# Splitting the first chunk's product at 288 tokens and regating four loads in a fused attention and ReLU-squared kernel

## Chip, cores and metric

The kernel runs on one core of one Trainium2 chip. The time is device time in microseconds (us). Before the change the median of 13 runs is 321.25 us (319.57 to 327.11). In the profiles, PE is TensorE's matrix multiply and PEld its weight load, DVE is VectorE, ACT is ScalarE, POOL is GpSimd and SP is SyncE, which here only issues DMAs.

## What is computed

Eight batch rows of attention, 576 tokens and 8 heads of 64 each, followed by a two-layer product with a squared ReLU between. Heads 0 to 3 see a sliding window of 32 tokens, heads 4 to 7 the same 32 places at a distance of four tokens.

```python
scores = scale * np.matmul(q, k.transpose(0, 1, 3, 2))
rel = pos[:, None] - pos[None, :]
mask_plain = (rel >= 0) & (rel < 32)
mask_dil = (rel >= 0) & (rel < 128) & (rel % 4 == 0)
attn = softmax(np.where(masks, scores, -1e9))
x = (attn @ v).transpose(0, 2, 1, 3).reshape(4608, 512)
h = x @ w_in                    # 512 x 2048
return np.maximum(h, 0.0) ** 2 @ w_out   # 2048 x 512
```

## The kernel before

The order of all instructions is written out by hand; each engine runs its own in that order, and waits on semaphores where data or a buffer is not there yet.

**Rows and chunks.** Attention goes by batch row `b` (576 tokens), the two products by chunk `c` (512 tokens). Chunk `c` can be multiplied once row `c` is done, so the product of chunk `b - 1` is interleaved with the attention of row `b`. A product is a Python generator in the list `pending`; `pump(n)` advances it by `n` steps, and TensorE's order is what these calls write down between the pieces of the attention.

**The products.** `mm1_gen` makes the hidden layer: for each of 16 columns of 128 of `w_in`, four matmuls over 512 tokens (L302) fill a PSUM tile `ph`, ScalarE's ReLU empties it into `rt` (L290), and VectorE squares two columns at once into `g` (L294). It yields twice a column. For chunk 0 the second product is `mm2_by_rows_gen` (64 matmuls, L323, in four blocks of `w_out`), for all later chunks `mm2_strassen_gen` (seven half-size products, L350, 28 steps), which needs sums of `g` that VectorE makes (L279 to L282) and differences of `w_out` (`weight_sums`, L271).

**Attention of rows 0 and 1.** `load_sliding_qk` brings q and k of the sliding heads to `sq` in float32, and `cast_sliding_qk` makes float16 of them; `load_dilated_qk` brings those of the dilated heads to `nd_` (the tile `early` in the profile). TensorE transposes them (`t_sliding` L475, `t_dilated` L489; the copies out of PSUM are L145 on ScalarE and L147 on VectorE), scores come from `s_sliding` (L514) and `s_dilated` (L551), each with an Exp on ScalarE (L504) and a mask on VectorE (L505). `av_sliding` (L583) and `av_dilated` (L597) multiply with v, VectorE normalizes (L565, L566), and `x_sliding` (L612) and `x_dilated` (L630) transpose the result into `xT`, the input of the first product, 288 tokens at a time. v comes as float32 in `sv` (6 loads of 256-byte pieces) and `sd` (2 loads), and is cast to `vp` and `vd`. Score and value tiles share two PSUM buffers (`papool`), everything else four (`pmool`): a third score tile waits for the Exp of the first.

**Rows 2 to 7.** q and k are copied in DRAM to float16 (`keep_qk`, tile `dk`, on GpSimd's queue), and `transpose_by_dma` brings them transposed to `QKTx` and `QKTd` (SP's queue, L194 and L196). `s_sliding_x` (L532) scores the sliding heads.

**Loads and who lets them go.** SP's queue carries, in this order, q and k of row 0 and v of row 0, q, k and v of row 1, v of row 2, the transposes of row 2, v of row 3 and so on. GpSimd's queue carries the dilated q and k, `w_in` (L128), `w_out` (L135), `dk` and the stores of the output; GpSimd also casts, so a load stands behind the casts that are written before it. `w_in` stands behind the first cast of row 0's v, `w_out` behind row 1's four casts of q and k (`cast_sliding_qk(1, (nc.gpsimd,) * 4)`). `dk` of row 2 stands behind `nc.gpsimd.memset(hold, 0.0)`, which waits for a VectorE write of `hold` made in the second value step of row 1; the loads of row 1 wait in the same way for two VectorE writes to `sq` and `nd_` (L698, L699).

**Order of the start.** Row 0's attention is filled with idle matmuls on zeros (`idle`, L450), which do nothing but keep TensorE going. Only after all of row 0 comes `mm1_gen(0)`: 22 steps alone, the other ten between the transposes and scores of row 1 (`begin(1, ...)`), then `mm2_by_rows_gen(0)` between the values of row 1. v of row 1 is cast on GpSimd.

Of the kernel before, what the change touches and what calls it, by code (L numbers as in the profile page):

```python
# [17 lines left out]
def kernel(  # L18
# [107 lines left out]
    def load_w_in():  # L126
        for f0, f1 in ((0, 1024), (1024, 2048)):
            nc.gpsimd.dma_start(  # L128
                out=wi[:, :, f0:f1],
                in_=moe_w_in[:, f0:f1].rearrange("(dh dl) f -> dl dh f", dl=P),  # L130
            )
# [17 lines left out]
    def cast_sliding_qk(b, engs):  # L149
        for i in (1, 0):  # L150
            for half in range(2):
                j0 = 3 * half
                copy(
                    engs[2 * i + half],
                    nq_[:, i, j0 : j0 + 3, :, :],
                    sq[:, i, :, D * j0 : D * (j0 + 3)].rearrange("p h (j d) -> p j h d", d=D),
                )

    def cast_sliding_v(eng, step, m0=0, m1=NB):
        for m in range(m0, m1, step):  # L160
            copy(eng, vp[:, m : m + step, :, 0:D], sv[:, m : m + step, :, :])

    def cast_dilated_v(eng, step):
        for t in range(2):
            for c in range(0, DIL, step):
                copy(
                    eng,
                    vd[:, t, c : c + step, :, 0:D],
                    sd[:, t, :, D * c : D * (c + step)].rearrange("p h (c d) -> p c h d", d=D),
                )  # L170

    def cast_v(eng):
        cast_sliding_v(eng, NB)
        cast_dilated_v(eng, DIL)
# [110 lines left out]
    def relu_squared(c, ffc, g, ph, rts):  # L285
        i, o = divmod(ffc, 2)
        if o == 0:
            rts[i] = osb.tile([P, 2, TOKC], FP16, name=f"rt{c}_{i}", tag="rt")
        rt = rts[i]
        nc.scalar.activation(rt[:, o, :], ph[:], ACTF.Relu)  # L290
        if i == NK - 1:
            nc.vector.tensor_mul(g[:, ffc, :], rt[:, o, :], rt[:, o, :])
        elif o == 1:
            nc.vector.tensor_mul(g[:, ffc - 1 : ffc + 1, :], rt, rt)  # L294

    def mm1_gen(c, g, sm=None):
        xs = xT[:, :, c * TOKC : (c + 1) * TOKC]
        rts = {}
        for ffc in range(NFF):
            ph = pmool.tile([P, TOKC], FP32, name=f"ph{c}_{ffc}", tag="pm")  # L300
            for dmk in range(NDM):
                nc.tensor.matmul(  # L302
                    ph,
                    wi[:, dmk, ffc * P : ffc * P + P],
                    xs[:, dmk, :],
                    start=(dmk == 0),
                    stop=(dmk == NDM - 1),
                )
# [129 lines left out]
    def hidden(c):  # L438
        return gp.tile([P, NFF, TOKC], FP16, name=f"g{c}", tag="g")
# [45 lines left out]

    def t_dilated(b, g, i, wide=False, eng=None):
        p_ = pt(f"pd{b}_{g}_{i}", wide)
        for j in range(6):
            nc.tensor.transpose(  # L489
                p_[:, QB * j : QB * (j + 1)],  # L490
                nd_[:, i, g, P * j : P * (j + 1)],
                ident[0:QB, 0:QB],
            )
        for a in range(2):
            copy(
                eng or (nc.vector if i else nc.scalar),
                QKTd[:, i, a, KPAD + 2 * g * CL : KPAD + 2 * (g + 1) * CL].rearrange(
                    "x (h p s) -> x h p s", h=2, s=3
                ),
                p_[:, 0:UW].rearrange("x (s a h p) -> x a h p s", a=2, h=2, p=48)[:, a],  # L500
            )
# [136 lines left out]
            py[:, 0:UW].rearrange("x (c r i) -> x c i r", c=2, r=DIL),  # L638
        )

    def begin(b, fill, wide=False):
        for hp in range(2):
            for i in (1, 0):
                t_sliding(b, hp, i, wide)
                fill()
        for g in range(2):
            s_sliding(b, g)
            fill()
            for i in (1, 0):
                t_dilated(b, g, i, wide, eng=nc.scalar)  # L650
                fill()
        for g in range(2):
            s_dilated(b, g)
            fill()

    def attn_values(b, fill, wide=False):
        xs = []
        for mp in range(3):
            xs.append(av_sliding(b, mp))
            fill()  # L660
        x_sliding(b, 0, xs, wide)
        fill()
        ys = [av_dilated(b, 0, 0)]
        fill()
# [10 lines left out]
        x_dilated(b, 1, zs, wide)  # L675


    cast_sliding_qk(0, (nc.scalar, nc.scalar, nc.vector, nc.gpsimd))
    cast_sliding_v(nc.gpsimd, 2, 0, 2)
    load_w_in()  # L680
    cast_sliding_v(nc.gpsimd, 2, 2, NB)
    cast_dilated_v(nc.gpsimd, 2)
    pj = pmool.tile([P, TOKC], FP32, name="pj", tag="pm")
    idle_matmuls(pj, 14, TOKC)
    n_idle = [0]

    def idle():
        n_idle[0] += 1
        idle_matmuls(pj, 5, P)

    begin(0, idle)

    def idle_and_load():
        idle()
        if n_idle[0] == 15:
            nc.vector.memset(sq[:, :, :, 0:1], 0.0)  # L698
            nc.vector.memset(nd_[:, :, :, 0:1], 0.0)  # L699

    attn_values(0, idle_and_load)
    load_sliding_qk(1)
    load_v(1)
    load_dilated_qk(1)
    cast_sliding_qk(1, (nc.gpsimd,) * 4)
    load_w_out()
    cast_sliding_v(nc.gpsimd, 2)
    cast_dilated_v(nc.gpsimd, 2)
    g0 = hidden(0)
    pending.append(mm1_gen(0, g0))  # L710
    pump(22)
    begin(1, lambda: pump(1))
    pump(1000)
    pending.append(mm2_by_rows_gen(0, g0))
    pump(4)
    n_val = [0]
    hold = const.tile([P, 1], FP32, name="hold")

    def rows_and_load():
        pump(2)  # L720
        n_val[0] += 1
        if n_val[0] == 2:
            nc.vector.memset(hold, 0.0)

    attn_values(1, rows_and_load, True)

    nc.gpsimd.memset(hold, 0.0)
    dk = keep_qk(2)
    load_v(2)
    transpose_by_dma(dk)  # L730
    pump(1000)
# [2 lines left out]
    for b in range(2, B):  # L734
        pending.append(moe_gen(b - 1))
        pump(1)
        if 2 < b < B - 1:
            dk = keep_qk(b + 1)
        if b == 2:

            for i in range(2):
                nc.gpsimd.tensor_copy(hold, QKTx[:, i, PADP + HH * S - 2 : PADP + HH * S - 1])
                nc.gpsimd.tensor_copy(hold, QKTd[:, i, 1, KPAD + S - 1 :])
            dk = keep_qk(b + 1)
            for _ in weight_sums():
                pump(2)
            cast_v(nc.scalar)
            load_v(b + 1)
            pump(4)
        else:  # L750
            pump(11)
        for g in range(2):
            s_sliding_x(b, g)
            pump(5)
        s_dilated(b, 0)
        pump(5 if b == 2 else 10)
        s_dilated(b, 1)
        if b + 1 < B:
            transpose_by_dma(dk)
        pump(4)  # L760
        attn_values(b, lambda: pump(2))
        if b + 1 < B:
            cast_v(nc.scalar)
        if b + 2 < B:
            load_v(b + 2)
        pump(1000)
# [33 lines left out]
```

## Time and profile before

| | us |
|---|---|
| median of 13 runs | 321.25 |
| the profiled execution, its own time | 320.37 |
| its span on the core | 318.2 |
| first product of chunk 0 begins | 28.04 |
| second product of chunk 0 begins | 50.32 |
| first product of chunk 1 begins (row 2's stage) | 68.22 |
| a row of the steady part (row 4, 134.6 to 166.5) | 31.9 |
| TensorE busy in it | 31.00 |

All times in the profile count from the start of the span. "Busy" is the time in which at least one instruction of an engine is under way; matmuls are pipelined, so the rate is read from the distance between them (one of 512 columns each 0.216 us at full clock). A number in square brackets behind a row of the timeline is the idle time of that engine before it, with what ended it. DMA shares are shares of 16 DMA engines; a share times the length of its window is called here the load's work, in us of all 16 engines.

### The profile page before, as it was taken

How to read it: one execution, taken by the hardware profiler on the slowest of the kernel's cores; microseconds unless marked ns; L12 is line 12 of the kernel's file. 1: busy time of each engine (PE TensorE's matmuls, PEld its weight loads, DVE VectorE, ACT ScalarE, POOL GpSimd, SP SyncE). 2: the span in 40 equal slices, each digit the busy share in tenths (PEclk: the TensorE clock that was granted, in tenths of full speed). 3: DMA queues.
4: the chain of work that ended last, by engine and by line, in shares of the span. 5: the costliest groups of instructions: out<-in, count | busy, mean ns of one | idle time of the engine just before them, and what ended most of it. 6: DMA issues, size and time to landing. Idle time of an engine off the chain costs nothing.

```text
span 318.2 us, 6930 instructions
## 1 busy us (share of the span) xinstructions
PE 297.8 (94%) x2876; PEld 195.2 (61%) x2876; DVE 212.0 (67%) x405; ACT 178.0 (56%) x302; POOL 47.9 (15%) x83
## 2 busy tenths in 40 slices
PE   6878887999999998999899989998999899999995
PEld 2866453544596457845784578447844784585484
DVE  4475576527987498748874887498749874844744
ACT  2565694168933982598259824982498236604620
POOL 4352590210202100030003000300000000000000
PEclk9599997999999999999999999999999999999999
DMA  7999999999997999199939992999330003003003
GB/s 187 234 181 225 213 194 202 238 204 232 226 205 179 221 207 191 24 266 204 197 39 268 206 182 50 268 196 203 38 135 0 2 2 132 0 2 132 2 0 132
DMA packets 83310, 47.89 MB, mean 150 GB/s; under 512 B 67792, under 2 KB 79568, under 8 KB 82896
## 3 DMA queue, kind: packets, MB, share of 16 engines
q1 hardware_dynamic: 75060, 26.12, 43.7%
q0 software_dynamic: 6848, 19.80, 28.2%
q10 hardware_dynamic: 1372, 1.54, 1.8%
q8 instruction: 22, 0.36, 0.5%
q14 instruction: 8, 0.07, 0.1%
HBM read 39.85 MB, written 16.52 MB: 177 GB/s over the span
## 4 chain that ended last, share of the span: by engine, by line
PE 71%; DVE 12%; ACT 7%; issue 4%; DMA 2%; POOL 2%; ACTq 0%; POOLq 0%
PE ph L302 32%; PE pob L350 9%; PE poa L350 6%; PE po L323 5%; PE poe L350 4%; PE poc L350 4%; DMA sq<-in_k_dram 2%; DVE AT L505 2%; PE paw L597 2%; ACT rt L290 2%; PE pod L350 2%; ACT QKTd L145 2%; ACT AT L504 2%; PE px L612 1%; DVE x_p L566 1%
## 5 line engine op out<-in xcount | busy, mean ns | idle before, releaser
L302 PE MATMUL ph<-xT,wi 128*128 128x512 f16 x576 | 131.2, 379 | 1.7 <-ACT rt L290 1.1
L290 ACT ACTIVATE rt<-ph 128x512 f16<-128x512 f32 x144 | 84.1, 606 | 28.3 <-PE ph L302 28.0
L302 PEld LDWEIGHTS <-wi 128*128 128x128 f16 x576 | 54.1, 98 | 63.4 <-issue 2.8
L294 DVE TENSOR_TENSOR g<-rt 128x1024 f16<-128x1024 f16 x63 | 45.0, 715 | 51.9 <-ACT rt L290 51.7
L350 PEld LDWEIGHTS <-sm 128*128 128x128 f16 x512 | 47.2, 98 | 5.0
L350 PEld LDWEIGHTS <-g 128*128 128x128 f16 x384 | 35.5, 98 | 5.3 <-DVE g L294 0.3
L618 ACT COPY xT<-px 128x576 f16<-128x576 f16 x16 | 10.2, 638 | 44.4 <-PE px L612 44.4
L350 PE MATMUL pob<-T,sm 128*128 128x256 f16 x256 | 32.5, 272 | 0.0
L350 PE MATMUL poa<-wo,g 128*128 128x256 f16 x256 | 31.9, 273 | 0.1
L370 POOL DMA_DIRECT2D out_dram<-otl x6 | 4.5, 756 | 159.2 <-DVE otl L405 140.7
L636 ACT COPY xT<-py 128x576 f16<-128x576 f16 x16 | 10.2, 638 | 30.1 <-PE py L630 30.1
L566 DVE TENSOR_TENSOR x_d<-paw,rcp_d 72x512 f16<-72x512 f32 x32 | 22.0, 686 | 1.1
L505 DVE TENSOR_TENSOR AT<-AT,maskp 128x576 f16<-128x576 f16 x32 | 17.5, 561 | 4.3 <-ACT AT L504 3.6
L504 ACT ACTIVATE AT<-ps 128x576 f16<-128x576 f32 x32 | 19.3, 664 | 0.6 <-PE ps L514 0.3
L504 ACT ACTIVATE AT<-pz 128x576 f16<-128x576 f32 x32 | 19.3, 681 | 0.0
L450 PE MATMUL pj<-zz 128*128 128x128 f16 (+1 forms) x124 | 16.5, 277 | 1.2 <-DVE zz L208 1.2
L323 PE MATMUL po<-wo,g 128*128 128x512 f16 x64 | 17.0, 402 | 0.0
L566 DVE TENSOR_TENSOR x_p<-pav,rcp_p 96x512 f16<-96x512 f32 x24 | 16.5, 687 | 0.8
L350 PE MATMUL poc<-T,sm 128*128 128x256 f16 x128 | 16.3, 272 | 0.0
L350 PE MATMUL pod<-T,g 128*128 128x256 f16 x128 | 16.1, 272 | 0.0
L350 PE MATMUL poe<-wo,sm 128*128 128x256 f16 x128 | 15.5, 273 | 0.0
L583 PE MATMUL pav<-vp,AT 128*128 128x65 f16 x192 | 10.1, 194 | 5.2 <-DVE x_p L566 4.5
(89 smaller groups left out, 328.0 us busy)
## 6 DMA issues: line engine op xcount, KB each, us to landing
sv<-in_v_dram SPq DMA_DIRECT2D x40, 128.0 KB, 8.7
sd<-in_v_dram SPq DMA_DIRECT2D x7, 512.0 KB, 10.9
dk<-in_k_dram POOLq DMA_DIRECT2D x12, 288.0 KB, 6.9
dk<-in_q_dram POOLq DMA_DIRECT2D x12, 288.0 KB, 8.8
out_dram<-otl POOLq DMA_DIRECT2D x6, 512.0 KB, 3.5
out_dram<-otu POOLq DMA_DIRECT2D x6, 512.0 KB, 4.3
wi<-in_moe_w_in_dram POOLq DMA_DIRECT2D x2, 1024.0 KB, 10.8
wo<-in_moe_w_out_dram POOLq DMA_DIRECT2D x4, 512.0 KB, 10.7
```

Of the source, the lines that this page charges most:

```text
L290: nc.scalar.activation(rt[:, o, :], ph[:], ACTF.Relu)
L294: nc.vector.tensor_mul(g[:, ffc - 1 : ffc + 1, :], rt, rt)
L302: nc.tensor.matmul(ph, wi[:, dmk, ffc * P : ffc * P + P], xs[:, dmk, :], start=(dmk == 0), stop=(dmk == NDM - 1),)
L323: nc.tensor.matmul(po, g[:, ffc, t * P : (t + 1) * P], wo[:, ffc, :], start=(ffc == 0), stop=(ffc == NFF - 1),)
L350: nc.tensor.matmul(acc, lhs[:, k, t * P : (t + 1) * P], rhs[:, k, :], start=(first and k == 0), stop=(k == NK - 1), skip_group_check=True,)
L450: nc.tensor.matmul(pj[:, 0:cols], zz[:, 0:P], zz[:, 0:cols], start=True, stop=True)
L504: nc.scalar.activation(AT[:, u, 0:UW], ps[:, :, 0 : UW // 2], ACTF.Exp, scale=scale)
L505: nc.vector.tensor_mul(AT[:, u, 0:UW], AT[:, u, 0:UW], mask)
L566: nc.vector.tensor_tensor(out=x[0:w], in0=pv[:, :, :, 0:D], in1=rcp[0:w].unsqueeze(3).to_broadcast([w, 2, HH, D]), op=ALU.mult,)
L583: nc.tensor.matmul(pav[:, i, h * (D + 2) : h * (D + 2) + D + 1], AT[:, u, off : off + P], vp[:, m, h, 0 : D + 1], start=True, stop=True,)
L618: nc.scalar.copy(xT[:, 0:2, t0 : t0 + 288], px[:, 0:UW].rearrange("x (c t) -> x c t", c=2),)
L636: nc.scalar.copy(xT[:, 2:4, t0 : t0 + 288].rearrange("x c (i r) -> x c i r", r=DIL), py[:, 0:UW].rearrange("x (c r i) -> x c i r", c=2, r= ...
```

## The change

The start is written anew; the functions of attention and of the later products stay, but for one new generator. `begin` becomes `transposes_and_scores` and `scores_dilated`.

- `mm1_part_gen` does the first product for a part of a chunk's tokens, one step a column. Chunk 0 goes in a part of 288 tokens, which is begun when the first 288 tokens of row 0 are in `xT`, and one of 224. The value steps of row 0 are reordered for it.
- `w_in` is let go by a VectorE write behind row 0's first two sliding masks, `w_out` by one behind the twelfth column of part one, `dk` and v of row 2 by writes in row 1's second value step (and `keep_qk(2)` moves into that step).
- Row 0's v is cast after `w_in` is issued, dilated heads first. Row 1's q and k are cast by ScalarE and VectorE after three columns of part two. Row 1's v is cast by ScalarE after the last column of part two and ahead of the Exp of row 1's dilated scores. Row 1's transposes use the four-buffer pool.
- In row 2's stage the sliding scores come four steps later (`pump(8)`), in rows 3 to 7 the second dilated score comes three steps sooner (7 for 10) and the values two steps later in all (9 for 4 behind it).

```diff
+    def mm1_part_gen(c, g, t0, t1):
+        xs = xT[:, :, c * TOKC + t0 : c * TOKC + t1]
+        rt = None
+        for ffc in range(NFF):
+            ph = pmool.tile([P, TOKC], FP32, name=f"ph{c}_{ffc}_{t0}", tag="pm")
+            for dmk in range(NDM):
+                nc.tensor.matmul(
+                    ph[:, 0 : t1 - t0],
+                    wi[:, dmk, ffc * P : ffc * P + P],
+                    xs[:, dmk, :],
+                    start=(dmk == 0),
+                    stop=(dmk == NDM - 1),
+                )
+            o = ffc % 2
+            if o == 0:
+                rt = osb.tile([P, 2, TOKC], FP16, name=f"rt{c}_{ffc}_{t0}", tag="rt")
+            nc.scalar.activation(rt[:, o, 0 : t1 - t0], ph[:, 0 : t1 - t0], ACTF.Relu)
+            if o == 1:
+                r = rt[:, :, 0 : t1 - t0]
+                nc.vector.tensor_mul(g[:, ffc - 1 : ffc + 1, t0:t1], r, r)
+            yield
...
-    cast_sliding_v(nc.gpsimd, 2, 0, 2)
-    load_w_in()
-    cast_sliding_v(nc.gpsimd, 2, 2, NB)
-    cast_dilated_v(nc.gpsimd, 2)
...
     def idle_and_load():
         idle()
-        if n_idle[0] == 15:
-            nc.vector.memset(sq[:, :, :, 0:1], 0.0)
-            nc.vector.memset(nd_[:, :, :, 0:1], 0.0)
-
-    attn_values(0, idle_and_load)
+        n_idle[0] += 1
+        if n_idle[0] == 5:
+
+            nc.vector.memset(hold, 0.0)
+            nc.gpsimd.memset(hold, 0.0)
+            load_w_in()
+            cast_dilated_v(nc.gpsimd, 2)
+            cast_sliding_v(nc.gpsimd, 2)
+
+    n_idle = [0]
+    transposes_and_scores(0, idle_and_load)
+    scores_dilated(0, idle)
+    xs = [av_sliding(0, 0)]
+    idle()
+    xs.append(av_sliding(0, 1))
+
+    nc.vector.memset(sq[:, :, :, 0:1], 0.0)
+    nc.vector.memset(nd_[:, :, :, 0:1], 0.0)
+    idle()
+    ys = [av_dilated(0, 0, 0)]
+    idle()
+    x_sliding(0, 0, xs, False)
+    idle()
+    ys.append(av_dilated(0, 0, 1))
+    idle()
+    xs.append(av_sliding(0, 2))
+    idle()
+    x_dilated(0, 0, ys, False)
     load_sliding_qk(1)
     load_v(1)
     load_dilated_qk(1)
-    cast_sliding_qk(1, (nc.gpsimd,) * 4)
+
+
+    g0 = hidden(0)
+    pending.append(mm1_part_gen(0, g0, 0, 288))
+    zs = []
+    for a in range(2):
+        pump(1)
+        zs.append(av_dilated(0, 1, a))
+    pump(1)
+    x_sliding(0, 1, xs, False)
+    pump(2)
+    x_dilated(0, 1, zs, False)
+    pump(8)
+    nc.vector.memset(hold, 0.0)
+    nc.gpsimd.memset(hold, 0.0)
     load_w_out()
-    cast_sliding_v(nc.gpsimd, 2)
-    cast_dilated_v(nc.gpsimd, 2)
-    g0 = hidden(0)
-    pending.append(mm1_gen(0, g0))
-    pump(22)
-    begin(1, lambda: pump(1))
     pump(1000)
+    pending.append(mm1_part_gen(0, g0, 288, TOKC))
+    pump(3)
+    cast_sliding_qk(1, (nc.scalar, nc.vector, nc.scalar, nc.vector))
+    pump(2)
+    transposes_and_scores(1, lambda: pump(1))
+    pump(1000)
+    cast_v(nc.scalar)
     pending.append(mm2_by_rows_gen(0, g0))
-    pump(4)
+    pump(3)
+    scores_dilated(1, lambda: pump(3))
     n_val = [0]
...
         if n_val[0] == 2:
             nc.vector.memset(hold, 0.0)
-
+            nc.vector.memset(sv[:, :, :, 0:1], 0.0)
+            nc.vector.memset(sd[:, :, :, 0:1], 0.0)
+            nc.gpsimd.memset(hold, 0.0)
+            dks.append(keep_qk(2))
+
+    dks = []
     attn_values(1, rows_and_load, True)
-
-    nc.gpsimd.memset(hold, 0.0)
-    dk = keep_qk(2)
+    dk = dks[0]
     load_v(2)
     transpose_by_dma(dk)
     pump(1000)
...
             cast_v(nc.scalar)
             load_v(b + 1)
-            pump(4)
+            pump(8)
...
         s_dilated(b, 0)
-        pump(5 if b == 2 else 10)
+        pump(5 if b == 2 else 7)
         s_dilated(b, 1)
         if b + 1 < B:
             transpose_by_dma(dk)
-        pump(4)
+        pump(4 if b == 2 else 9)
         attn_values(b, lambda: pump(2))
```

More of the change, by code (lines that the diff above doesn't have):

```diff
@@ L639, in x_dilated, with transposes_and_scores @@
         )
-    def begin(b, fill, wide=False):
+    def transposes_and_scores(b, fill):
         for hp in range(2):
             for i in (1, 0):
-                t_sliding(b, hp, i, wide)
+                t_sliding(b, hp, i)
                 fill()
@@ L649, in begin, with scores_dilated @@
             for i in (1, 0):
-                t_dilated(b, g, i, wide, eng=nc.scalar)
+                t_dilated(b, g, i, eng=nc.scalar)
                 fill()
+    def scores_dilated(b, fill):
         for g in range(2):
@@ L675, in attn_values @@
         x_dilated(b, 1, zs, wide)
+    hold = const.tile([P, 1], FP32, name="hold")
     cast_sliding_qk(0, (nc.scalar, nc.scalar, nc.vector, nc.gpsimd))
-    cast_sliding_v(nc.gpsimd, 2, 0, 2)
-    load_w_in()
-    cast_sliding_v(nc.gpsimd, 2, 2, NB)
-    cast_dilated_v(nc.gpsimd, 2)
     pj = pmool.tile([P, TOKC], FP32, name="pj", tag="pm")
     idle_matmuls(pj, 14, TOKC)
-    n_idle = [0]
     def idle():
-        n_idle[0] += 1
         idle_matmuls(pj, 5, P)
-    begin(0, idle)
     def idle_and_load():
         idle()
-        if n_idle[0] == 15:
-            nc.vector.memset(sq[:, :, :, 0:1], 0.0)
-            nc.vector.memset(nd_[:, :, :, 0:1], 0.0)
-    attn_values(0, idle_and_load)
+        n_idle[0] += 1
[23 more added lines that the diff above has]
+    x_dilated(0, 0, ys, False)
     load_sliding_qk(1)
@@ L704 @@
     load_dilated_qk(1)
-    cast_sliding_qk(1, (nc.gpsimd,) * 4)
-    load_w_out()
-    cast_sliding_v(nc.gpsimd, 2)
-    cast_dilated_v(nc.gpsimd, 2)
-    g0 = hidden(0)
-    pending.append(mm1_gen(0, g0))
-    pump(22)
-    begin(1, lambda: pump(1))
-    pump(1000)
+    g0 = hidden(0)
[11 more added lines that the diff above has]
+    nc.gpsimd.memset(hold, 0.0)
+    load_w_out()
+    pump(1000)
+    pending.append(mm1_part_gen(0, g0, 288, TOKC))
[5 more added lines that the diff above has]
+    cast_v(nc.scalar)
     pending.append(mm2_by_rows_gen(0, g0))
-    pump(4)
+    pump(3)
+    scores_dilated(1, lambda: pump(3))
     n_val = [0]
-    hold = const.tile([P, 1], FP32, name="hold")
     def rows_and_load():
```

## The prediction

> **What bounds the kernel now.** The page first: busy time, and the 40 slices of 8 us.
>
> ```profile
> PE 297.8 (94%) x2876; PEld 195.2 (61%) x2876; DVE 212.0 (67%) x405; ACT 178.0 (56%) x302; POOL 47.9 (15%) x83
> ...
> PE   6878887999999998999899989998999899999995
> ...
> DMA  7999999999997999199939992999330003003003
> ```
>
> TensorE is the bound from row 2 on; in the first six slices it has holes, while the DMA engines are full. So the start is read by the timeline, where each row gives start, duration, what, and the idle time before:
>
> ```profile
> 14.80 1.54 POOL L128 DMA_DIRECT2D wi<-in_moe_w_in_dram  x2
> ...
> 28.93 9.23 PE L302 MATMUL ph<-xT,wi 128*128 128x512 f16 x42 [0.29 <-ACT xT L636]
> ...
> 39.79 3.02 POOL L135 DMA_DIRECT2D wo<-in_moe_w_out_dram  x4
> ...
> 49.42 0.97 PE L551 MATMUL pz<-QKTd 64*128 64x72 f16 x16 [2.43 <-ACT AT L504]
> 50.32 3.16 PE L323 MATMUL po<-wo,g 128*128 128x512 f16 x8
> ...
> 77.38 0.43 PE L532 MATMUL ps<-QKTx 64*128 64x96 f16 x12
> ```
>
> At 49.42 TensorE had stood 2.43 us for the Exps of row 1's dilated scores. The windows of 3.41 us (busy of each engine, then clock, DMA share, GB/s) show what that cost:
>
> ```profile
> 46.07:49.48 3.41, 0.98 (x24) 0.52 (x23) 3.11 (x7) 3.41 (x10) 1.59 (x2) 1.00 1.18 191
> 49.48:52.90 3.42, 3.28 (x23) 1.37 (x23) 1.75 (x4) 1.59 (x3) 0.00 (x0) 0.50 1.22 198
> ```
>
> Half the clock in the next window: eight matmuls take 3.09 us in the chain of waits, 1.73 at full clock, some 1.5 us lost with the scores. Then the DMA queues while `w_out` (q0, GpSimd's) and row 2's v (q1, SP's) load together, 48 to 54:
>
> ```profile
> q0 software_dynamic: 928, 0.92, 90.8%
> q1 hardware_dynamic: 926, 0.23, 29.2%
> ```
>
> As many packets each, but v's are 256 bytes: `w_out` gets three parts in four. Last, what TensorE waits for from 102 to 290:
>
> ```profile
> PE pav L583 <- DVE x_p L566: 4.5, 5, 0.9
> PE ph L302 <- ACT rt L290: 0.6, 1, 0.6
> ```
>
> Once in each of rows 3 to 7 the third value tile waits 0.9 us for VectorE, which is late by its sums and masks.
>
> **The start, up to the last column of chunk 0.** `w_in` no longer waits for a cast of v but for two masks, which end at 15.5; with 0.4 us from a VectorE `hold` to a DMA behind it (55.76 to 56.13) it is issued at 15.9 instead of 14.8. It landed 13.5 us after issue at most, so by some 30. Row 0's values are paced by VectorE (0.85 us a tile, after the masks end at 21.6): the fourth is done at 25.5, `x_dilated` and its copy take 1.1, and part one begins at 26.65 instead of 28.04. Its matmuls have 288 columns, by the 512-column step of 0.216 us some 0.121 each, 0.485 a column. Four value and transpose pieces (0.27 each) lie between, so column 8 begins at 31.6, after `w_in`, and part one ends at 35.5. By then the kernel before had done 32 of its 64 matmuls (7.0 us of work), this one 7.8: the 288 tokens gain 0.8 us, no more, since they take the place of idle matmuls only from 26.65.
>
> Part two runs against ScalarE. Row 1's k landed by 35.8 and I take the same. From 37.1 ScalarE has 2 casts (1.56 for two at 7.60), 13 ReLUs of 224 columns (0.25 each; bounds 0.25 and 0.50, the latter the distance of 512-column ones at 81.1), 2 copies (0.54), 4 Exps (0.56) and 8 copies of 288 (0.32; four took 1.34 at 17.52): 10.6 us, and 0.7 for TensorE's waits, so 48.4. TensorE reaches `mm2` at 47.4 (its first block needs only four columns), does ten matmuls and the first dilated scores, and stands at 50.3 before the second: both score buffers wait for Exps, and these now stand behind the casts of row 1's v on ScalarE.
>
> **When row 1's v lands.** The twelfth column of part one ends at 33.6, VectorE squares it by 34.4, and `w_out` is issued at 34.7 instead of 39.79. Before, v had the engines nearly alone then. The loads' work (share times window, us of 16 engines):
>
> ```profile
> q0 software_dynamic: 2112, 2.10, 81.2%
> ...
> q1 hardware_dynamic: 3794, 1.50, 39.1%
> ```
>
> `w_out` (41 to 57): 13.0. One row of v (47 to 66): 7.4. Of v about 0.7 is done when `w_out` starts at 36.4 (its first packets came 1.7 after issue before). The 256-byte part, 3.7, goes at the 0.30 of the row above: until 48.7. `w_out` has then 1.9 left; the 1024-byte part shares with it (I take packet for packet, 0.47 and 0.70) to 51.4, and ends at 53.3. Together they need 20 at 1.2, which gives 53.1: as long as v is the one that waits, the end is fixed. Landing 0.6, the last cast 1.05 (77.18, two in 1.99), an Exp 0.6: TensorE goes on at 55.6. It has stood 5.3 us. Were v's share even, it would go on at 52.4 (casts of 3.4 from 48.4, then the Exp).
>
> From there 54 matmuls (11.7), the scores (0.3) and the eight value and four transpose pieces (2.8): 14.8. After so long a wait the clock is halved; at the start of the span, where matmuls resumed at 9.17, it stayed at half until about 15.3, so I take 4.2 us at half, 2.1 lost (bounds 0.9 and 3.4). Row 2's stage begins at 72.5 instead of 68.4: **+4.1** (+0.3 with even shares).
>
> The Trainium skill ("DMA: Bandwidth & Descriptors", "Rules for kernel authors") says to issue a DMA early and wait late. By that rule the earlier `w_out` costs nothing and the sum is that of the first rival. The rows speak against it, because the engines are shared and the earlier load is not the one that is waited for.
>
> **Row 2.** `dk` and v of row 2 are let go in the second value step, at 62.2 by the halved clock, instead of 56.13 for `dk` and 43.45 for v; between 53.3 and then the DMA engines have nothing to load. Before `QKTx` is there, they must do `dk` (5.7: 65.9% of 58 to 66.6), v (7.4; it is ahead of the transposes on SP's queue), the two stores of chunk 0 (3.5: 43.9% of 69 to 77) and some 6.6 of transposes (of 82.0% of 66 to 77.2, less v's share, two thirds): 23.2 at 1.15, from 63.9 until 84.1, and 0.9 to land. TensorE comes there after 12.5 columns (10.8) and the 0.9 that it waits behind the casts of v: 84.3. That is **+0.7** (0 to 2); `pump(8)` has bought the rest. At the end of the stage its four steps are missing as filler: the last values wait for VectorE 1.6 us and the copy 0.9. Against that stand holes that the earlier mm1 no longer has; my sum over the stage is **-0.2**. But 2.45 us of idle time in 2.75 is as much as halved the clock at 49.48; it may fall into two windows, so **+0.8** (0 to 1.7).
>
> The Trainium skill ("TensorE: Matmul & The Clock Gate", "What's actually happening") has the clock halved after an idle window of about 3.4 us. By that rule the 5.3 us halve it and the 2.45 don't, and the sum is 0.8 less; here 2.43 us with 0.98 busy in the window were enough, so I keep the term.
>
> **Rows 3 to 7.** The second dilated score comes 3 steps sooner, so its two masks (0.74 together at 153.47) fill VectorE's holes before the sums; the values come 2 steps (8 matmuls of 0.109, 0.87 us) later against the product. The 0.9 goes. At the end 8 matmuls instead of 16 cover ScalarE's casts of 3.4 us: the fifth `ph` of the next chunk would have had 0.8 us of slack and now waits about 0.15. Five times 0.75: **-3.7** (-4.5 to -2.5).
>
> GpSimd's casts (4.05 us for q and k, 0.65 each for v) go; they cost nothing but the waits already counted.
>
> **Sum.** 4.1 + 0.7 - 0.2 + 0.8 - 3.7 = +1.7 on the profiled span of 318.2 (its own time 320.37). The median is 0.9 over that run; the difference goes onto it: 322.95, say 323.0. By their bounds, the terms put this case at 321.0 to 325.5.
>
> **Rivals.**
> - *Faster: v lands in time.* If q1 gets an even share, or the small part flows ahead, TensorE goes on at 52.4 and the stage at 68.7; `dk` is let go near 57.5 and `QKTx` lands as TensorE arrives. 0.3 - 0.2 - 3.7 = -3.6: 317.6. For it: shares with 1024-byte pieces are unmeasured, v is split in two. Against: the 29.2%. It decides if v's last landing is before 50.
> - *Slower still: the steady rows don't gain.* If VectorE's sums move by as much as the values, or the next chunk's columns wait 0.9 for the casts, the 3.7 are lost: 326.7. For it: in row 3 the casts already cost 0.58 (105.91). Against: VectorE's holes of 0.6 us before the sums.
> - *It does not do what it says: `w_in` late.* Starting 1.1 later and meeting row 1's q, its second half could land at 33; column 8 waits 1.4, `w_out` is let go as much later, v comes sooner by about that: 321.5.
>
> **How the numbers follow.** The forecast 0.51, faster rival 0.31, slower 0.13, late `w_in` 0.05. A measurement here tells 0.3% (1.0 us) from no change. Of the forecast's case 0.09 lies within that, 0.42 above; of the late `w_in` 0.03 within, 0.02 on the faster side. Faster 0.33, same 0.12, slower 0.55. The range takes in both sides: 317.0 to 327.0, with some 0.1 left out at each end.
>
> **What would show it.** The second scores `pz` of row 1 with an idle time of about 5 us ended by an Exp, ScalarE waiting on `sv` and `sd`; the clock at half around 53 to 60; no wait of `pav` for `x_p` in rows 3 to 7; row 2's first product at about 72.5. If v lands before 50 or the steady rows are still 31.9 apart, the prediction is wrong.

## Result and profile after

The changed kernel takes 325.62 us (median of 11 runs, 321.59 to 336.12) against 320.91 us of the kernel before beside it (48 runs). The ratio is 1.0118, with a 95% interval of 1.0087 to 1.0149: slower by 0.9 to 1.5%. The ratio leaves out executions more than 1.5% above the fastest of the same kernel, so it lies below the quotient of the medians (1.0147). The profiled execution took 325.94 us with a span of 324.0, where the one before had 320.37 and 318.2.

The 5.8 us between the two spans, by stages (a row's stage begins with the first matmul of the first product that is interleaved with the row, that of the chunk before):

| stage | before, us | after, us | difference | forecast |
|---|---|---|---|---|
| start to row 2's stage | 68.22 | 72.59 | +4.37 | +4.1 |
| row 2's stage | 33.04 | 37.66 | +4.62 | +1.3 (0.7 - 0.2 + 0.8) |
| row 3's | 33.15 | 33.00 | -0.15 | -0.75 |
| rows 4 to 7, each | 31.95 | 31.19 | -0.76 | -0.75 |
| the rest | 55.98 | 56.00 | 0.0 | 0 |

("The rest" is what comes behind row 7's stage, the products of the last two chunks.) What TensorE waited for in the changed kernel, 40 to 115 us (in total, times, longest), and then 102 to 296:

```profile
PE pz L573 <- ACT AT L526: 5.1, 2, 4.9
PE ps L554 <- DMA QKTx<-dk: 2.3, 1, 2.3
PE py L652 <- DVE x_d L588: 1.1, 1, 1.1
```

```profile
PE py L652 <- DVE x_d L588: 1.1, 1, 1.1
PE ph L324 <- ACT rt L290: 0.6, 4, 0.2
PE ph L324 <- ACT xT L658: 0.3, 1, 0.3
```

The wait of 0.9 us for `x_p`, once a row, is not in the second list: that is the gain of rows 4 to 7. The first list has the losses, one at row 1's dilated scores, two in row 2's stage. The timeline shows how the first comes about (start, duration, what; in brackets the idle time before and who ended it):

```profile
35.70 3.01 POOL L135 DMA_DIRECT2D wo<-in_moe_w_out_dram  x4
...
38.28 0.46 SPq L114 DMA_DIRECT2D sd<-in_v_dram  x1
...
51.65 1.04 ACT L145 CAST vd<-sd 128x1024 f16<-128x1024 f32 x1 [1.15 <-DMA sd<-in_v_dram]
54.67 1.04 ACT L145 CAST vd<-sd 128x1024 f16<-128x1024 f32 x1 [1.98 <-DMA sd<-in_v_dram]
...
56.32 0.30 PE L573 MATMUL pz<-QKTd 64*128 64x72 f16 x8 [4.91 <-ACT AT L526]
```

`w_out` is on its way 2.6 us before the last piece of row 1's v is issued. That piece lands 16.4 us later, its cast waits, the Exps wait behind the cast, and TensorE waits 4.91 us for an Exp. The second loss, on SP's queue and TensorE:

```profile
62.45 6.97 SPq L106 DMA_DIRECT2D sv<-in_v_dram  x6
...
72.18 12.14 SPq L194 DMA_TRANSPOSE QKTx<-dk  x2
...
87.00 0.50 PE L554 MATMUL ps<-QKTx 64*128 64x96 f16 x12 [2.31 <-DMA QKTx<-dk]
```

Each wait is followed by a half clock. In windows of 3.41 us (busy of PE, PEld, DVE, ACT, POOL with counts, then clock, DMA share, GB/s), laid on the edges at which the clock changed:

```profile
53.10:56.51 3.41, 0.19 (x8) 0.19 (x8) 0.21 (x1) 1.83 (x3) 0.00 (x0) 1.00 0.06 14
56.51:59.92 3.41, 3.17 (x25) 1.30 (x18) 1.62 (x4) 1.46 (x3) 0.00 (x0) 0.50 0.00 0
83.79:87.20 3.41, 0.80 (x12) 0.33 (x13) 2.64 (x5) 1.71 (x4) 0.22 (x1) 1.00 1.17 223
87.20:90.61 3.41, 3.41 (x19) 1.29 (x13) 1.37 (x3) 2.16 (x4) 0.50 (x1) 0.50 1.13 200
107.70:111.11 3.41, 1.88 (x28) 1.09 (x27) 2.29 (x6) 1.30 (x3) 1.52 (x3) 1.00 1.27 277
111.11:114.52 3.41, 3.38 (x9) 1.14 (x9) 0.00 (x0) 3.41 (x4) 1.52 (x4) 0.50 1.38 299
```

The first two rows also show idle DMA engines (share 0.06 and 0.00) where before v of row 2 was loading: it is not yet let go.

### The profile page after: what moved, and what is told of

It is laid out like the page before. It is cut to its first block, busy times and chain, and to the rows that moved or that the text cites. A ratio compares the mean times of both kernels' runs of the same rounds, so it can differ in the third digit from the quotient of the medians.

```text
span 324.0 us, 7034 instructions
## 1 busy us (share of the span) xinstructions
PE 300.2 (93%) x2920; PEld 200.8 (62%) x2920; DVE 214.5 (66%) x418; ACT 183.3 (57%) x323; POOL 39.1 (12%) x74
## 4 chain that ended last, share of the span: by engine, by line
PE 73%; DMA 10%; ACT 7%; DVE 5%; SPq 3%; issue 1%; ACTq 0%; POOL 0%
PE ph L324 28%; PE poa L372 9%; PE pob L372 9%; DMA sd<-in_v_dram 5%; PE pod L372 4%; PE poc L372 4%; PE po L345 3%; PE poe L372 3%; DMA QKTx<-dk 3%; DMA sq<-in_k_dram 2%; ACT vd L145 2%; PE paw L619 2%; SPq L194 2%; ACT vp L145 2%; DVE AT L527 2%; PE ph L302 2%
## 5 line engine op out<-in xcount | busy, mean ns | idle before, releaser
L324 PE MATMUL ph<-xT,wi 128*128 128x512 f16 x512 | 119.8, 387 | 1.9 <-ACT rt L290 1.6
L324 PEld LDWEIGHTS <-wi 128*128 128x128 f16 x512 | 49.0, 99 | 60.6 <-issue 7.9
L290 ACT ACTIVATE rt<-ph 128x512 f16<-128x512 f32 x128 | 73.3, 603 | 22.0 <-PE ph L324 21.6
L294 DVE TENSOR_TENSOR g<-rt 128x1024 f16<-128x1024 f16 x56 | 38.7, 690 | 45.7 <-ACT rt L290 45.5
L527 DVE TENSOR_TENSOR AT<-AT,maskd 128x576 f16<-128x576 f16 x32 | 14.2, 466 | 7.9 <-ACT AT L526 7.1
L302 PE MATMUL ph<-xT,wi 128*128 128x288 f16 (+1 forms) x128 | 16.8, 272 | 1.6 <-ACT rt L312 0.9
L372 PE MATMUL poe<-wo,sm 128*128 128x256 f16 x128 | 16.3, 273 | 0.0
```

Of the source, the lines that this page charges most:

```text
L302: nc.tensor.matmul(ph[:, 0 : t1 - t0], wi[:, dmk, ffc * P : ffc * P + P], xs[:, dmk, :], start=(dmk == 0), stop=(dmk == NDM - 1),)
L324: nc.tensor.matmul(ph, wi[:, dmk, ffc * P : ffc * P + P], xs[:, dmk, :], start=(dmk == 0), stop=(dmk == NDM - 1),)
L372: nc.tensor.matmul(acc, lhs[:, k, t * P : (t + 1) * P], rhs[:, k, :], start=(first and k == 0), stop=(k == NK - 1), skip_group_check=True,)
L527: nc.vector.tensor_mul(AT[:, u, 0:UW], AT[:, u, 0:UW], mask)
```

## Experiments

All ratios are against the kernel before, run beside each kernel. "Row 2 begins" is the start of its stage, all from the profiled execution:

| run | median, us | ratio (95%) | span | second product of chunk 0 begins | row 2 begins | row 2's stage | row 3's |
|---|---|---|---|---|---|---|---|
| before | 320.91 | | 318.2 | 50.32 | 68.22 | 33.04 | 33.15 |
| after | 325.62 | 1.0118 (1.0087, 1.0149) | 324.0 | 48.19 | 72.59 | 37.66 | 33.00 |
| steady_only | 316.45 | 0.9872 (0.9803, 0.9940) | 313.0 | 50.48 | 67.12 | 33.04 | 32.07 |
| wout_later | 324.92 | 1.0118 (1.0044, 1.0192) | 320.6 | 48.18 | 67.78 | 39.99 | 32.07 |
| exps_first | 322.78 | 1.0053 (1.0007, 1.0099) | 318.9 | 46.65 | 65.50 | 39.65 | 33.02 |
| row2_pump4 | 326.10 | 1.0168 (1.0088, 1.0248) | 322.2 | 48.58 | 69.84 | 39.52 | 32.08 |
| row2_qk_early | 317.49 | 0.9881 (0.9827, 0.9935) | 315.2 | 48.05 | 67.66 | 33.79 | 33.02 |
| row2_loads_early | 317.83 | 0.9896 (0.9861, 0.9931) | 314.1 | 45.49 | 65.09 | 34.13 | 33.02 |
| row2_early_fill | 316.98 | 0.9872 (0.9793, 0.9951) | 314.2 | 45.96 | 67.21 | 33.04 | 32.07 |
| row2_early_exps | 316.25 | 0.9849 (0.9796, 0.9902) | 313.6 | 47.79 | 66.65 | 33.04 | 32.07 |
| wout_early_row2_early | 326.83 | | 325.1 | 48.04 | 78.27 | 33.79 | 32.07 |
| unsplit_rest_kept | 313.68 | 0.9779 (0.9703, 0.9855) | 312.0 | 47.22 | 66.08 | 33.04 | 32.07 |
| casts_after_masks | 315.62 | 0.9837 (0.9765, 0.9909) | 314.2 | 48.39 | 67.25 | 33.04 | 32.07 |
| row1_qk_sooner | 314.56 | 0.9790 (0.9746, 0.9833) | 311.6 | 46.67 | 65.53 | 33.05 | 32.07 |

### The steady rows alone

The kernel before, with only the two counts of rows 3 to 7:

```diff
-        pump(5 if b == 2 else 10)
+        pump(5 if b == 2 else 7)
...
-        pump(4)
+        pump(4 if b == 2 else 9)
```

> The kernel before with only the step counts of rows 3 to 7 changed (7 for 10, 9 for 4). Theory: the wait of the third value tile for VectorE goes in all five rows (0.9 each) and the cover at the end costs some 0.1: a row of 31.2 us instead of 31.95, the whole 3.5 to 4 us faster than before (ratio 0.988). Rival, VectorE's sums only move along: rows stay at 31.95, ratio 1.00.

Measured: 0.9872, a row takes 31.19 to 31.20 us, and of the waits from 102 to 290 us

```profile
PE ph L302 <- ACT rt L290: 1.2, 5, 0.6
```

is all that is left. Two numbers of the change bring this, and by themselves they beat both kernels. Everything else in the change costs 9.2 us on top (325.62 less 316.45).

### `w_out` later

The three lines that let `w_out` go are moved from part one to behind the casts of row 1's q and k:

```diff
     pump(8)
-    nc.vector.memset(hold, 0.0)
-    nc.gpsimd.memset(hold, 0.0)
-    load_w_out()
     pump(1000)
...
     cast_sliding_qk(1, (nc.scalar, nc.vector, nc.scalar, nc.vector))
+    nc.vector.memset(hold, 0.0)
+    nc.gpsimd.memset(hold, 0.0)
+    load_w_out()
```

> The changed kernel with w_out let go after the casts of row 1's q and k, some 4 us later (near 40). Theory (the early w_out starves row 1's v): v lands by 43, the second dilated scores wait under 2 us instead of 4.9, row 2's stage begins near 68.5 instead of 72.6 and its first scores do not wait for QKTx; ratio to before 0.99. Rival (3.4 us of casts ahead of the Exps on ScalarE are the cost, whenever v lands): a wait of 3.5 us or more stays, row 2's stage not before 70.5, ratio 1.00 or more.

`w_out` is issued at 40.02 us and row 2's stage begins at 67.78, 4.8 us sooner: the first loss is what the forecast said it was. But the time does not fall. TensorE's waits in it, 40 to 115 us:

```profile
PE ps L554 <- DMA QKTx<-dk: 3.6, 1, 3.6
PE pz L573 <- ACT AT L526: 1.8, 2, 1.5
...
PE py L652 <- DVE x_d L588: 1.1, 1, 1.1
```

Row 2's stage grows from 37.66 to 39.99: TensorE comes to the scores sooner and waits longer, and two windows run at half clock (82.5 to 89.3). A second limit stood behind the first.

### Exps first

ScalarE's casts of row 1's v behind the dilated scores instead of ahead of them, `w_out` as early as in the change:

```diff
-    cast_v(nc.scalar)
     pending.append(mm2_by_rows_gen(0, g0))
     pump(3)
     scores_dilated(1, lambda: pump(3))
+    cast_v(nc.scalar)
```

> The changed kernel with the casts of row 1's v on ScalarE behind the Exps of the dilated scores; loads as in the change. Theory (v is late, but only what stands behind its casts suffers): the scores no longer wait, the first value tile waits 1 to 2 us, row 2's stage begins near 68; ratio to before 0.985 to 0.99. Rival (v late holds the values as long as it held the scores): the same 4 to 5 us appear before the first value tile, ratio 1.005 or more.

The wait for Exps is gone although `w_out` is still early (34.16 us) and the last piece of row 1's v still late (it lands at 52.4), and row 2's stage begins at 65.50. So the first loss needs both: a late v, and the Exps queued behind its cast. The time is still not below that of the kernel before, for the same reason as in the last run: a wait of 3.7 us for `QKTx`, a stage of 39.65.

### Row 2's fillers

`pump(4)` for `pump(8)` ahead of row 2's first scores, all else as in the change.

> The changed kernel with 4 steps instead of 8 before row 2's first scores. Theory (the four steps are missing as filler at the end of the stage, where TensorE then waits 1.1 and 0.3 us and gets half the clock): the first scores wait about 4 us for QKTx instead of 2.3, but the end of the stage has its fillers and full clock; row 3's stage begins 1 to 2 us earlier than 111.1 and runs 1.5 faster; ratio to before 1.004 to 1.008. Rival (QKTx's landing sets the stage, fillers are nothing): 1.012 as the change, or more.

The stage doesn't shorten to the old length. The wait for `x_dilated` at its end falls from 1.1 to 0.3 us, but the wait for `QKTx` is 6.7 us. The time that row 2's q and k need sets the stage, not the fillers. (The start of this kernel is the changed kernel's, yet in its profile row 1's v came in time: TensorE waited 1.5 us for an Exp instead of 4.9, and row 2's stage began at 69.84. So the first loss doesn't come in every execution.) In all four kernels with `dk` let go behind row 1's second value step TensorE began those scores as soon as `QKTx` was there, and that was 24.4 to 25.8 us after the issue of `dk` (62.65 to 87.00 in the changed kernel, 57.85 to 83.44 in wout_later). In the kernel before it was 21.3 us at most (56.13 to 77.38, without a wait), and there v of row 2 had been issued at 43.45, ahead of `dk`.

### Row 2's loads early

From here on the base is wout_later. First `dk` alone is issued right behind `w_out`:

```diff
     load_w_out()
+    dks = [keep_qk(2)]
...
-            dks.append(keep_qk(2))
```

> As wout_later, and the load of row 2's query and key into SBUF (dk) is issued right behind w_out instead of after the second value step of row 1; row 2's values keep their gate. Theory (the late release of row 2's loads is what row 2's stage pays for: QKTx landed 23.7 to 24.9 us after that release in the changed kernel, wout_later, exps_first and row2_pump4 alike): dk has landed long before SyncE comes to the transposes, so QKTx lands some 5 us sooner, at 75 to 78 us with a stage beginning at 67.8; TensorE reaches those scores about 11 us into the stage, at 79, so the wait of 3.6 us for QKTx and the two half-clock windows behind it (82.5 to 89.3) go; row 3's stage begins at 102 to 104 instead of 107.8, span 315 to 316.5, ratio 0.985 to 1.000. Rival (the transposes themselves are slow behind the values, whatever the time of dk): QKTx still lands beyond 81, the wait stays above 2 us, span 319 to 321, ratio 1.00 to 1.015.

Then v of row 2 is no longer held back either:

```diff
-        n_val[0] += 1
-        if n_val[0] == 2:
-            nc.vector.memset(hold, 0.0)
-            nc.vector.memset(sv[:, :, :, 0:1], 0.0)
-            nc.vector.memset(sd[:, :, :, 0:1], 0.0)
-            nc.gpsimd.memset(hold, 0.0)
```

> As row2_qk_early, and the three writes that hold row 2's values back until the second value step go too, so that SyncE issues those values as soon as ScalarE's casts of row 1's have read the tiles, at about 50 us. Theory: values and transposes both come sooner, QKTx at 71 to 75 us, no wait at the scores (79), row 3's stage at 101.5 to 103.5, span 313 to 316, ratio 0.978 to 0.995. Rival (values loaded at 50 us take the DMA engines from what row 1 still needs): TensorE waits for row 1's query and key or values between 50 and 60 us, and row 2's stage begins at 69 or later instead of 67.8; ratio above 0.995.

With `dk` alone `QKTx` is there at 77.2 us (GpSimd, which reads a column of it, stops waiting then), and TensorE begins its scores at 79.68 without a wait, where it began at 83.44 in wout_later. SP's queue:

```profile
57.52 5.49 SPq L106 DMA_DIRECT2D sv<-in_v_dram  x6
...
64.10 10.29 SPq L194 DMA_TRANSPOSE QKTx<-dk  x2
```

The wait is gone, row 2's stage falls from 39.99 to 33.79 us and the ratio from 1.0118 to 0.9881. That settles the second loss: it hangs on when one load, four pieces of 288 KB, is let go. Letting v go too brought nothing more. TensorE began those scores at 77.60 after a wait of 0.4 us, so `QKTx` did not land at 71 to 75, and the ratio is the same.

### The fillers again, and the Exps again

On row2_loads_early, first `pump(4)` for `pump(8)`, then also `cast_v` behind the dilated scores (the two edits shown above).

> As row2_loads_early, with pump(4) for pump(8) ahead of row 2's first scores, so that four steps of the first product's filler move to the end of the stage. In row2_pump4 that made the wait for x_dilated at the end of the stage 0.3 us instead of 1.1 but brought TensorE to the scores 1 us sooner, where it waited for QKTx. Theory: with QKTx early the second cost is gone and only the gain is left: 0.8 us of wait and the half clock of some 3.4 us at the start of row 3's stage (1.7 us), so 1 to 2.5 us below row2_loads_early. Rival (row 2's stage is its sum of work, filler placed earlier or later is the same): within 0.5 us of row2_loads_early.

> As row2_early_fill, with ScalarE's casts of row 1's values behind row 1's dilated scores instead of ahead of them. In exps_first that moved row 2's stage from 72.6 to 65.5 us, against 67.8 with the later w_out alone. Theory: row 2's stage at 65 to 67 and 1 to 2 us below row2_early_fill, as long as QKTx (then wanted at 76.5) has landed. Rival (the casts then end later, row 2's values and the transposes behind them with them): QKTx lands above 77, a wait of over 1 us at the scores comes back, and the time is that of row2_early_fill or more.

Now that nothing waits for `QKTx`, the fillers do what row2_pump4 could not show: the stage falls from 34.13 to 33.04, and row 3's from 33.02 to 32.07, as the wait at the end of the stage is 0.3 instead of 1.1 us and the clock stays up. The medians (317.83 and 316.98) differ by less than their intervals; the profile of row2_early_fill has a half-clock window at the start (52.3 to 55.7) that row2_loads_early's lacks, so their spans are level. The Exps shorten the way from the second product of chunk 0 to row 2's stage from 19.60 us (in wout_later, row2_qk_early and row2_loads_early alike) to 18.86, and the values wait 1.1 us for their cast instead; the medians differ by 0.7 us, less than was expected.

### Do the two losses add?

row2_loads_early with `w_out` let go where the change has it, at the end of part one.

> As row2_loads_early (span 314.1, row 2's stage at 65.1, 249.0 us from there to the end), with the load of w_out let go where the change has it, at the end of part one instead of behind row 1's casts; row 2's query and key stay behind the casts. It asks whether the two costs add. Theory (w_out ahead of row 1's values costs row 1 some 4 us by itself; row 2's own cost comes from its loads alone): row 1's values land beyond 52 us, TensorE waits 3.5 us or more at row 1's dilated scores, row 2's stage begins at 70 to 72.5 and then lasts 33.5 to 34.5 as in row2_loads_early; span 319 to 321.5, ratio 1.000 to 1.008. Rival (row 2's loads are pushed back by w_out too, so the stage is longer again): row 2's stage beyond 36 us, span above 322.

Row 2's stage takes 33.79 us, as in row2_qk_early (34.13 in row2_loads_early), so its loss has nothing to do with `w_out`. But in the profile the first loss doubled, against both theories:

```profile
59.38 1.04 ACT L145 CAST vd<-sd 128x1024 f16<-128x1024 f32 x1 [7.90 <-DMA sd<-in_v_dram]
```

TensorE waits 9.8 us. GpSimd issues `dk` at 38.5 to 40.6, straight behind the early `w_out`, and row 1's v now shares the engines with both. From 53 to 58 us, with `w_out` nearly done and `dk` under way on q0, next to nothing is left for the last of v on q1:

```profile
q0 software_dynamic: 155, 1.11, 105.0%
q1 hardware_dynamic: 190, 0.07, 6.3%
```

That `dk` is the reason is read from these rows; no run separates it from row 2's v, which is let go at 50.4 here. The four times were 327.09, 326.58, 320.73 and 327.42 us, too uneven for a ratio. The profile is of the first. The third, with a span of 318.7, is 4.6 us above row2_loads_early's span, about what the theory gave, so the doubled loss is not shown for every execution either.

### The split alone

row2_early_exps with the first product of chunk 0 in one piece behind row 0:

```diff
-    pending.append(mm1_part_gen(0, g0, 0, 288))
...
-    pump(8)
-    pump(1000)
-    pending.append(mm1_part_gen(0, g0, 288, TOKC))
-    pump(3)
+    pending.append(mm1_gen(0, g0))
+    pump(18)
     cast_sliding_qk(1, (nc.scalar, nc.vector, nc.scalar, nc.vector))
...
-    pump(2)
+    pump(4)
```

(and `idle()` for the steps between row 0's last values)

> As row2_early_exps (span 313.6 in its profile, row 2's stage at 66.65), but the first product of chunk 0 stays in one piece of 512 tokens behind row 0's last values, as in the kernel before, with idle matmuls in the places of part one's steps, and about as many of its steps left for row 1's transposes. Theory (part one fills TensorE's time between row 0's last values and is worth what those gaps are, some 0.8 to 1.3 us): row 2's stage at 67.4 to 68.0, span 314.3 to 315.0, ratio 0.987 to 0.992. Rival (the split gains nothing once the loads come in time, because 2 x 16 steps of 288 and 224 tokens cost more weight loads and evictions than 16 of 512): row 2's stage at 66.7 or sooner, span 313.6 or less.

By the absolute times the rival holds. The first product begins at 28.49 instead of 25.85 us, and yet row 1's first transposes begin at 38.45 instead of 38.31, the second product at 47.22 instead of 47.79. The time is the lowest of all. But the two profiles differ before the edit can act: row 0's first value tile begins at 18.68 us here and at 20.13 in row2_early_exps, with the same instructions up to there. From that tile to row 2's stage it takes 47.40 us without the split and 46.52 with it. And more than the split differs behind it: without it TensorE runs at half clock from 21.68 to 25.09 and waits 0.7 us for `w_out` and 0.9 for `QKTx`. How much of the 2.6 us between the medians is the split's is therefore open. Of the spans, 1.1 us lies behind the last matmul, where the span ends 4.3 us after the last store is issued in row2_early_exps and 3.3 in unsplit_rest_kept; 0.6 us is what the stages show (the last chunk's first product begins at 282.58 and 282.00).

Where the head start of the split goes can be followed in row2_early_exps. The four value and transpose pieces of row 0 that stand inside part one take 1.2 us, TensorE waits 0.5 for a copy into `xT`, and 0.86 for the cast of row 1's key. On ScalarE:

```profile
37.42 1.56 ACT L145 CAST early<-sq 96x768 f16<-96x768 f32 x2 [0.34 <-DMA sq<-in_k_dram]
```

The cast waits for the load of that key. So one more run keeps the split and lets row 1's q and k go sooner:

```diff
     scores_dilated(0, idle)
+    nc.vector.memset(sq[:, :, :, 0:1], 0.0)
+    nc.vector.memset(nd_[:, :, :, 0:1], 0.0)
     xs = [av_sliding(0, 0)]
     idle()
     xs.append(av_sliding(0, 1))
...
-    nc.vector.memset(sq[:, :, :, 0:1], 0.0)
-    nc.vector.memset(nd_[:, :, :, 0:1], 0.0)
```

> As row2_early_exps (split kept), with the two small VectorE writes that let row 1's query and key go placed ahead of row 0's normalizations instead of behind the first of them, some 2 us sooner. In row2_early_exps row 1's first transposes began at 38.31 us after a wait of 0.86 for the cast of that key, which itself waited for the landing; in unsplit_rest_kept, whose first product begins 2.6 us later, they began at 38.45. Theory (the split's head start ends at that landing): the key lands 1 to 2 us sooner, at 35.5 to 36.5, the wait of 0.86 us goes, row 1's transposes begin at 37.0 to 37.6, row 2's stage 0.7 to 1.5 us sooner relative to the start of part one (40.8 us behind it before: 39.3 to 40.1), and the time falls by as much, ratio 0.980 to 0.984. Rival (the DMA engines are full then: the share was 1.0 to 1.1 from 24 to 48 us, so what lands sooner delays w_in or row 1's values): TensorE waits for w_in in part one or for the values by as much, and the ratio stays at 0.984 or above. Either way unsplit_rest_kept (0.978) stays ahead or level.

The load is issued 1.5 us sooner against the start of part one (3.2 us ahead of it instead of 1.7), the cast begins at 36.52 without a wait for it, row 1's transposes at 37.40, and from the start of part one to row 2's stage it takes 40.13 us instead of 40.80. The ratio is 0.979. But the sooner load is not shown to be the reason. casts_after_masks, whose load stands where row2_early_exps has it, takes the same 40.13 us. In seven of the eleven kernels with the split, row1_qk_sooner among them, row 1's transposes begin 12.0 us behind part one, after a wait of 0.40 for the cast:

```profile
37.40 0.49 PE L497 MATMUL pt<-ident,early 96*128 96x96 f16 x6 [0.40 <-ACT early L145]
```

In row2_early_exps it was 12.46. So its key was late as in few of the others, and the landing is not what commonly ends the head start. The time is level with no split at all (314.56 and 313.68 us): these runs show no gain of the split in the time, and which of the two is faster stays open.

### VectorE against GpSimd's casts

In the changed kernel one of VectorE's masks of row 0 took 3146 ns. GpSimd's seven casts of row 0's v begin at the same moment (17.42 and 17.43 us). In row2_early_exps a read of the fourth mask's output is put ahead of those casts:

```diff
+        if n_idle[0] == 8:
+            nc.gpsimd.tensor_copy(hold, AT[:, 3, 0:1])
             cast_dilated_v(nc.gpsimd, 2)
             cast_sliding_v(nc.gpsimd, 2)
```

> As row2_early_exps, with GpSimd's seven casts of row 0's values begun only after VectorE's fourth mask, by a read of one column of that mask's output ahead of them. In four of the eight traces with the split a mask that began within 0.2 us of the first of those casts took 3.0 to 3.3 us, in the others 0.7 to 0.9. Theory (VectorE stands still while GpSimd's casts run back to back): the first four masks take 0.45 to 0.5 us each, none above 1.0, the next four up to 0.9 as they still meet casts; the values are cast 1 to 1.5 us later, at 23 us, and TensorE waits for them, so the time is that of row2_early_exps within 0.3% or up to 1 us above. Rival (the long mask has to do with the load of w_in that GpSimd has just issued, not with its casts): a mask of over 2 us is still among the first four.

The masks, shortest, median and longest in ns, in the changed kernel and then in this one:

```profile
L527 DVE TENSOR_TENSOR AT<-AT,maskp x4: 458/657/3146, 14.8 to 20.5; 128x576 f16<-128x576 f16 x4
```

```profile
L527 DVE TENSOR_TENSOR AT<-AT,maskp x4: 457/457/459, 14.1 to 16.9; 128x576 f16<-128x576 f16 x4
```

All four take 0.46 us now, as the theory has it. With the casts ungated one of the first four took 0.7 us or more in each of the eleven profiles of kernels that cast row 0's v behind `w_in`. But four of these have no mask above 0.9 either, so one profile without a long mask doesn't rule out the load of `w_in` for the long one. The time stays where it was (0.9837 beside 0.9849): the values are cast later and TensorE waits 1.2 us for them.

## Why the forecast was right, and where it was not

The direction was right, and 325.62 lies in the range of 317 to 327, but 0.1 us outside the likeliest case's own 321.0 to 325.5. The range is wide and takes in both signs: the forecast was 1.7 us more, and the time grew by 4.7.

- **The start, +4.1; measured +4.37.** The mechanism holds, and in the profiled execution the size. The last landing of v was put at 53.3 to 53.9, its cast began at 54.67; TensorE was to go on at 55.6 and went on at 56.32; the wait was put at 5.3 and was 4.91. The half clock behind it was put at 2.1 us lost and was one window of 3.41, 1.7 lost, so two small misses cancel. The forecast saw both links, the load and the casts ahead of the Exps, and wout_later and exps_first show that taking away either ends it.
- **"The 288 tokens gain 0.8 us" does not hold.** The forecast had part one done by 35.5 us, 7.8 us of work against 7.0. At 35.5 us the changed kernel had begun 57 of its 64 matmuls, 6.9 us of work at 0.121 each, and the kernel before 33 of its own, 7.1. Part one began 0.27 us later than summed, and behind its first two matmuls it waited 0.48 us for a copy into `xT`, which the sum doesn't have (the row below). Row 1's key, taken to land by 35.8 as before, landed at 37.7; ScalarE came to its cast at 38.04 and did not wait. The second product did begin 2.1 us sooner than before (48.19), but without the split it begins at 47.22 in the one profile there is, so these runs don't tell how much of the 2.1 is the split's.

```profile
27.81 0.40 PE L302 MATMUL ph<-xT,wi 128*128 128x288 f16 x2 [0.48 <-ACT xT L658]
```

- **Row 2, "+0.7 (0 to 2)" with "-0.2" and "+0.8 (0 to 1.7)": the step that failed, in size.** The mechanism was named: `dk` let go at 62.2 (62.65 on the timeline), v ahead of the transposes, TensorE at 84.3 (84.7). The landing, summed up to 85.0, came at 87.0, 2.31 us late instead of 0.7. The largest single part is the clock. The forecast had one half-clock window as possible, at the end of the stage, and priced it at less than half of its bound; two came, one behind the `QKTx` wait (some 1.7 us in the stage) and one behind the wait for `x_dilated` at its end (0.93 us, row 3's 33.00 against 32.07 in row2_early_fill). The fillers taken from the end cost 0.75 us (33.79 in row2_qk_early against 33.04), where the sum had put the stage's own balance at -0.2. Together 2.3 + 1.7 + 0.75 is 4.75, beside 4.62 measured.
- **Rows 3 to 7, -3.7; measured -3.2.** Rows 4 to 7 gave 0.76 each. Row 3 lost its share to the half clock just named.
- **The rivals.** "v lands in time" was real in row2_pump4, whose v casts found their data at 49.15 to 51.5 us without a wait. Its start is the changed kernel's, so it is in part luck which of the two cases a profile shows. There the last piece of v was issued 1.1 us behind `w_out`, in the changed kernel 2.6 and in exps_first 2.4, where v was late too. That this margin decides is read from the profiles and not tested. "`w_in` late" did not show: no wait for `w_in` stands in TensorE's list. "The steady rows don't gain" is ruled out by steady_only.
- **The rule of the Trainium skill to issue a DMA early and wait late** ("DMA: Bandwidth & Descriptors", "Rules for kernel authors") cut both ways here. For `dk` it paid, 6.2 us of row 2's stage; for `w_out` it cost 4.8 (row 2's stage at 72.59 against 67.78 in wout_later), since another load was needed first.

## What to carry to other kernels

Where the DMA engines are full, issuing a load earlier delays the ones that are in flight, so write down which load is wanted first and let them go in that order; a gate that keeps a load off one stage must not make the next stage wait for it. When a wait is removed, work out which landing is next before booking the gain: here `QKTx` swallowed nearly all that the later `w_out` had gained. And price a wait with the half clock that may follow it.

## What the runs showed of the hardware

- **Half a window of idle time can be enough to halve the clock.** In the changed kernel TensorE was busy 1.88 of 3.41 us (107.70 to 111.11) and the next window ran at 0.50; in row2_qk_early the same with 1.84 (99.50 to 102.91). Laid on the same edges over all 14 profiles, up to 310 us, each of the 23 full-speed windows with 1.64 us busy or less was followed by half speed, and each of the 1150 with 2.17 or more by full speed. Of the 23 between them 7 were followed by half speed, with up to 2.11 busy (casts_after_masks, 16.37 to 19.78), and 16 by full speed, with as little as 1.66 (the changed kernel, 22.38 to 25.79). What decides there is open. The Trainium skill ("TensorE: Matmul & The Clock Gate", "What's actually happening") names an idle window of about 3.4 us. Here a window far from empty was enough.
- **VectorE can lose to a whole run of GpSimd's instructions.** In seven of the eleven profiles of kernels with those casts ungated, a mask of 0.46 us took 3.0 to 3.5 while casts of 0.60 to 0.83 ran back to back; in the other four the two took turns and a mask took 0.7 to 0.9. TensorE then waited 1.9 to 2.1 us for row 0's `x_p` in the seven, 0.6 to 1.2 in the four. The Trainium skill ("SBUF — State Buffer", "SBUF: two separate sides") has a VectorE instruction with two SBUF inputs and a GpSimd instruction lock each other out for the length of one instruction. That agrees with the turns; a mask that stands through about five casts is more than one instruction's worth. Which of the two happens, these runs don't tell.
